# A new order of all steps, down to single second-layer matmuls, in a fused attention and feed-forward kernel

## The chip, the core and the metric

The kernel runs on one core of a Trainium2 chip. The core has five engines that each take their own instructions in the order in which the program issues them: TensorE (PE, matmuls; its weight loads are shown as PEld), VectorE (DVE), ScalarE (ACT), GpSimd (POOL) and SyncE (SP, which here only issues DMAs). The metric is the time on the device, in microseconds (us), as the median of several runs.

## The reference

There are two parts. Attention between a sequence `x` (8 batches, 8 heads, 512 positions, 64 features) and a small `state` (32 rows) runs both ways; its two results are put under each other (544 rows a batch), the heads side by side (512 columns), and a two-layer block with a periodic activation is applied to all 4352 rows:

```python
scores = scale * x @ state^T;   a  = softmax(scores);  xread = a @ state     # 512 rows a batch
scores2 = scale * state @ x^T;  a2 = softmax(scores2); sread = a2 @ x        # 32 rows a batch
X = concat([xread, sread]), heads to columns                                 # 4352 x 512
h = X @ w_in                                                                 # 512 -> 2048
g = h + sin(alpha * h)**2 / (alpha + 1e-9)
out = g @ w_out                                                              # 2048 -> 512
```

## The kernel before

The program is a long string, `ORDER`, of steps with their arguments, and a class `Steps` with a method for each. The body reads `ORDER` from left to right and calls the method; nothing is rearranged afterwards, so the string fixes the order on each engine, and the framework adds the waits that the data and the buffers need. A letter at a step's end chooses its engine (A ScalarE, V VectorE, G GpSimd). Eight PSUM banks are given out by hand: a step that opens a bank names it, and it waits until the bank's last user is done.

The work goes by batch. `xread @ w_in` is not computed as it stands: the softmax weights times (state times `w_in`) give the same, so for every batch a matrix M (256 x 2048) takes the place of `w_in`, and the first layer of 512 positions has a depth of 256.

- Loads: `li.s` and `lo.s` bring the four slices of `w_in` and `w_out` (slice s holds the columns or rows of f = 4s to 4s+3), `lx.b` the x of batch b, all from GpSimd's DMA queue, which turns them to bf16 on the way. `lq` brings the x of batch 0 from SyncE's queue and `xq` casts it.
- x transposed: for batch 0 by TensorE (`xtq`, copied by `xc`), for batch 1 by TensorE too (`xt`, `xc`), for batches 2 to 7 by a DMA (`td`) from a packed copy that `pk` makes.
- Scores and weights: `sc` (matmul), `ex` (exp), `rs`, `rr` (sum, reciprocal), `nm` (normalise: a multiply of two SBUF tensors), then a transpose of the weights: `at`, `ac` for batch 0, a DMA `ad` for the others.
- M: `m.b.s` makes a piece of 512 columns in two banks by 8 matmuls of 64 x 32 tiles; `me` casts it to bf16.
- First layer: `h.t.f` makes 128 of the 2048 columns for the 512 positions of batch t by two matmuls (`hg.t.f.g` is one of the two, used for batch 0). t = 8 stands for the state rows of all batches together (256 columns, four matmuls). Then `si` (sine, ScalarE), `sq` (square, any engine; a multiply of two SBUF tensors on VectorE and GpSimd), `gt` (VectorE; gives the bf16 tile gT and frees the bank of h).
- Second layer: `o.t.st.f0.f1` adds the products of f0 to f1-1 into the bank of 128 output rows (st); 16 make a tile. `oc` copies it to one of six buffers, `os` stores it from SyncE's queue. The last tile, t 7 st 3, is made in two parts of 384 and 128 columns (`oh`, `och`, `osh`).
- The other direction: `w`, `cs` (matmuls), `rc`, `xs` put the state rows' inputs together.
- `warm_up.n.cols.bank` issues n matmuls on zeros whose result nobody reads.

All matmuls of the second layer are recorded at line 587, those of `h` at 537 and 543 (t = 8), of `hg` at 552, of `m` at 488, of `xt` at 376; the squares and the normalisations at line 201 (a helper), `si` at 560, `gt` at 576, `me` at 496, `oc` at 595, `os` at 602 (605 for t = 8).

Of the kernel before, what the change touches and what calls it, by code (L numbers as in the profile page):

```python
# [33 lines left out]
me.1.1.1.A warm_up.2.128.2 gt.0.2 si.0.0 warm_up.2.128.2 warm_up.2.128.6 warm_up.2.128.3
warm_up.2.128.2 warm_up.2.128.6 me.0.1.0.A gt.0.1 sq.0.0.G m.0.2.3.2 si.0.3 m.1.2.5.6 hg.0.4.0.7
me.0.2.0.V me.0.2.1.A hg.0.4.1 sq.0.3.G hg.0.6.0.4 me.1.2.1.V hg.0.6.1 si.0.4 hg.0.7.0.3 hg.0.11.0.2
me.1.2.0.V si.0.6 hg.0.7.1 sq.0.4.G hg.0.5.0.6 gt.0.0 hg.0.5.1 si.0.7 hg.0.11.1 hg.0.8.0.5 hg.0.8.1
sq.0.6.A gt.0.3 sq.0.7.G o.0.3.0.2.0 si.0.5 gt.0.4 o.0.3.2.3 o.0.0.0.2.1 si.0.11 o.0.0.2.3 gt.0.6
sq.0.5.G o.0.0.3.4 o.0.2.0.1.7 si.0.8 o.0.3.3.5 sq.0.11.A gt.0.7 hg.0.9.0.4 sq.0.8.G o.0.2.1.2
gt.0.5 o.0.2.2.4 hg.0.9.1 gt.0.11 o.0.0.4.5 hg.0.10.0.3 si.0.9 o.0.2.4.5 gt.0.8 o.0.0.5.6 o.0.3.5.6  # L40
sq.0.9.A o.0.3.6.8 pk.1.0.V hg.0.10.1 xt.1.1.6 pk.1.1.V si.0.10 gt.0.9 xt.1.0.2 xc.1.1.0.A sq.0.10.G
o.0.2.5.6 xc.1.1.1.V xc.1.0.0.A o.0.0.6.7 xc.1.0.1.V o.0.0.7.8 o.0.2.6.7 sc.1.1.5 gt.0.10 sc.1.0.4
m.0.3.6.2 ex.1.0 o.0.2.7.8 me.0.3.0.V o.0.1.0.3.3 me.0.3.1.V o.0.1.3.6 hg.0.13.0.6 o.0.1.6.7 ex.1.1
rs.1.0 hg.0.13.1 m.1.3.2.4 si.0.13 o.0.1.7.8 rr.1.0 rs.1.1 nm.1.0.0.4.G o.0.1.8.9 hg.0.12.0.5
o.0.3.8.9 rr.1.1 hg.0.12.1 me.1.3.0.V o.0.0.8.9 nm.1.1.0.4.G o.0.1.9.10 o.0.0.9.10 me.1.3.1.V
si.0.12 o.0.0.10.11 o.0.3.9.11 sq.0.13.G ad.1 hg.0.15.0.2 sq.0.12.A o.0.1.10.12 hg.0.15.1 gt.0.12
o.0.2.8.10 si.0.15 o.0.2.10.11 gt.0.13 o.0.0.11.12 hg.0.14.0.4 sq.0.15.A hg.0.14.1 o.0.3.11.13
si.0.14 gt.0.15 o.0.0.12.13 o.0.1.12.13 o.0.3.13.14 sq.0.14.A pk.2.0.V o.0.1.13.14 pk.2.1.V h.1.2.5
gt.0.14 h.1.4.6 td.2 si.1.2 lx.3.0.1 h.1.0.2 si.1.4 o.0.0.13.15 sq.1.2.V h.1.1.4 si.1.0 gt.1.2
sq.1.4.G o.0.3.14.16 si.1.1 o.0.2.11.13 sq.1.0.A oc.0.3.V h.1.6.5 sq.1.1.G gt.1.4 o.0.2.13.14 os.0.3  # L50
h.1.3.0 si.1.6 gt.1.0 o.0.1.14.16 si.1.3 sq.1.6.G h.1.13.6 gt.1.1 oc.0.1.A o.0.2.14.15 o.0.0.15.16
si.1.13 h.1.15.2 sq.1.3.G lx.4.0.1 gt.1.6 os.0.1 o.0.2.15.16 oc.0.0.A h.1.5.4 sq.1.13.V oc.0.2.V
si.1.15 h.1.7.3 os.0.0 gt.1.3 o.1.1.0.1.5 si.1.5 os.0.2 h.1.8.1 sq.1.15.G gt.1.13 o.1.1.1.2 si.1.7
o.1.2.0.2.7 sq.1.5.A o.1.1.2.3 sq.1.7.G h.1.12.0 gt.1.15 si.1.8 h.1.9.6 gt.1.5 o.1.2.2.3 si.1.12
sq.1.8.G o.1.2.3.5 gt.1.7 si.1.9 o.1.1.3.4 h.1.10.2 sq.1.12.A pk.3.1.V h.1.11.4 sq.1.9.G gt.1.8
o.1.2.5.6 si.1.10 o.1.2.6.7 gt.1.12 h.1.14.3 si.1.11 sq.1.10.G o.1.2.7.8 gt.1.9 sc.2.1.1 si.1.14
o.1.1.4.7 sq.1.11.A pk.3.0.V sq.1.14.G o.1.1.7.8 gt.1.10 td.3 o.1.2.8.9 sc.2.0.0 o.1.1.8.9 gt.1.11
o.1.1.9.10 ex.2.0 o.1.3.0.2.6 gt.1.14 o.1.3.2.4 o.1.2.9.10 o.1.3.4.5 o.1.2.10.12 ex.2.1 o.1.2.12.13
rs.2.0 o.1.1.10.11 m.2.2.2.4.3.0 rr.2.0 rs.2.1 o.1.2.13.14 nm.2.0.0.4.G me.2.3.0.A o.1.2.14.15 w.0.1
rr.2.1 me.2.2.1.A me.2.3.1.V o.1.3.5.6 nm.2.1.0.4.G me.2.2.0.A o.1.3.6.7 o.1.2.15.16 cs.0 oc.1.2.A  # L60
m.2.0.3.4.0.2 ad.2 rc.0 o.1.3.7.8 me.2.1.1.A o.1.3.8.9 sc.3.0.7 xs.0.1 me.2.1.0.A o.1.1.11.12 os.1.2
me.2.0.0.V sc.3.1.2 me.2.0.1.A o.1.1.12.13 o.1.3.9.10 xs.0.0 pk.4.1.V pk.4.0.V td.4 o.1.3.10.11
ex.3.0 o.1.1.13.16 ex.3.1 rs.3.0 o.1.3.11.13 oc.1.1.A o.1.3.13.14 rr.3.0 h.2.0.0 rs.3.1 nm.3.0.0.4.G
os.1.1 o.1.3.14.16 si.2.0 rr.3.1 h.2.1.3 oc.1.3.V nm.3.1.0.4.G h.2.2.4 h.2.8.1 os.1.3 h.2.3.7 ad.3
si.2.2 o.1.0.0.3.2 si.2.8 sq.2.0.V o.1.0.3.4 sq.2.2.G gt.2.0 h.2.4.5 si.2.1 o.1.0.4.6 si.2.3
sq.2.8.G o.1.0.6.7 gt.2.2 h.2.9.6 si.2.4 o.2.3.0.1.0 o.1.0.7.8 sq.2.1.G o.1.0.8.9 sq.2.3.A gt.2.8
o.1.0.9.10 h.2.5.4 si.2.9 gt.2.3 o.1.0.10.11 sq.2.4.G o.1.0.11.12 si.2.5 h.2.7.1 gt.2.1 o.1.0.12.13
sq.2.9.A sq.2.5.G o.1.0.13.14 gt.2.4 o.1.0.14.15 si.2.7 o.1.0.15.16 o.2.0.0.1.7 gt.2.9 o.2.0.1.2
oc.1.0.A h.2.6.3 sq.2.7.G gt.2.5 o.2.3.1.2 os.1.0 o.2.3.2.3 si.2.6 h.2.10.5 o.2.3.3.4 sq.2.6.A
o.2.3.4.5 gt.2.7 h.2.11.6 si.2.10 h.2.12.2 gt.2.6 si.2.11 o.2.0.2.3 sq.2.10.G o.2.0.3.4 o.2.3.5.6  # L70
si.2.12 h.2.15.4 h.2.13.1 sq.2.11.A gt.2.10 sq.2.12.G o.2.0.4.5 si.2.15 h.2.14.3 gt.2.11 o.2.3.6.7
si.2.13 o.2.0.5.6 sq.2.15.G gt.2.12 o.2.0.6.8 si.2.14 o.2.3.7.9 sq.2.13.A o.2.3.9.10 gt.2.15
sq.2.14.G o.2.0.8.11 gt.2.13 o.2.0.11.12 sc.4.0.5 sc.4.1.6 gt.2.14 o.2.3.10.12 ex.4.0 o.2.3.12.13
w.1.2 cs.1 o.2.0.12.13 rc.1 o.2.3.13.15 ex.4.1 o.2.3.15.16 m.3.0.4.1.3.5 rs.4.0 oc.2.3.A o.2.0.13.14
me.3.1.0.A o.2.0.14.15 os.2.3 me.3.0.0.V o.2.1.0.1.6 me.3.0.1.A o.2.1.1.2 o.2.0.15.16 rr.4.0 rs.4.1
o.2.1.2.3 me.3.1.1.A nm.4.0.0.4.G h.3.1.0 oc.2.0.A o.2.1.3.4 rr.4.1 xs.1.0 m.3.2.3.4.1.5 si.3.1
nm.4.1.0.4.G os.2.0 xs.1.1 h.3.0.7 me.3.2.0.V h.3.2.2 ad.4 me.3.3.0.V o.2.1.4.6 lx.5.0.1 o.2.2.0.1.3
me.3.3.1.V si.3.2 o.2.2.1.3 si.3.0 h.3.6.1 sq.3.1.V sq.3.2.G me.3.2.1.V h.3.14.5 si.3.6 o.2.2.3.4
gt.3.1 o.2.2.4.5 sq.3.0.G si.3.14 o.2.2.5.7 gt.3.2 o.2.2.7.8 sq.3.6.A o.2.2.8.9 h.3.8.4 sq.3.14.G
gt.3.0 h.3.5.0 si.3.8 gt.3.6 h.3.15.2 si.3.5 o.2.2.9.10 sq.3.8.G gt.3.14 o.2.2.10.11 h.3.9.7 si.3.15  # L80
h.3.7.1 si.3.9 sq.3.5.G gt.3.8 o.2.2.11.13 si.3.7 h.3.10.5 sq.3.9.G o.2.2.13.14 sq.3.15.A gt.3.5
o.2.2.14.15 h.3.4.4 si.3.10 gt.3.15 o.2.1.6.7 sq.3.7.G o.2.1.7.8 si.3.4 o.2.2.15.16 o.2.1.8.10
sq.3.10.A gt.3.9 o.2.1.10.11 sq.3.4.G gt.3.7 o.2.1.11.13 oc.2.2.A o.2.1.13.14 gt.3.10 o.2.1.14.16
os.2.2 h.3.3.0 gt.3.4 oc.2.1.A h.3.12.2 si.3.3 pk.5.1.V o.3.2.0.1.7 os.2.1 m.4.2.1.3.5.6 pk.5.0.V
si.3.12 sq.3.3.V td.5 o.3.3.0.1.4 me.4.2.1.V me.4.2.0.A o.3.2.1.2 sq.3.12.G o.3.3.1.2 me.4.3.0.A
o.3.2.2.3 gt.3.3 o.3.3.2.3 h.3.11.1 me.4.3.1.A gt.3.12 h.4.10.3 si.3.11 h.4.9.5 si.4.10 h.4.12.0
sq.3.11.V h.4.11.6 si.4.9 gt.3.11 sq.4.10.G o.3.2.3.5 si.4.12 o.3.2.5.7 sq.4.9.A o.3.2.7.8 gt.4.10
sq.4.12.G o.3.2.8.10 si.4.11 o.3.2.10.11 gt.4.9 o.3.3.3.5 sq.4.11.A o.3.3.5.6 gt.4.12 o.3.3.6.8
m.4.0.2.1.3.5 gt.4.11 o.3.3.8.9 me.4.1.1.V me.4.0.1.A h.3.13.0 me.4.0.0.A h.4.8.6 me.4.1.0.V
h.4.15.1 si.3.13 h.4.2.5 si.4.8 sq.3.13.V h.4.1.2 lx.6.0.1 si.4.2 gt.3.13 o.3.2.11.12 o.3.1.0.2.3  # L90
si.4.15 o.3.1.2.3 sq.4.8.V o.3.1.3.4 sq.4.2.G si.4.1 gt.4.8 o.3.3.9.12 sq.4.15.A h.4.3.0 sq.4.1.G
gt.4.2 o.3.3.12.13 h.4.13.6 si.4.3 gt.4.15 o.3.3.13.15 si.4.13 sq.4.3.G o.3.3.15.16 gt.4.1 h.4.6.5
# [65 lines left out]
class Steps:  # L158
# [449 lines left out]
    def oh(k, t, st, half, bank):  # L608
        k.o(t, st, 0, k.FT, bank, half=half)
# [54 lines left out]
```

## Time and profile before

| | |
|---|---|
| median of 3 runs | 221.4 us (221.1 to 221.64) |
| the profiled execution | 221.22 us, its span 219.2 us |
| TensorE busy | 211.4 us (96%), 1593 matmuls recorded |
| ScalarE, VectorE, GpSimd busy | 173.4, 162.9, 106.2 us |
| granted TensorE clock | 1.00 |
| second-layer matmuls (L587) | 542 recorded, 133.9 us |
| squares and normalisations on GpSimd (L201) | 91, mean 1.02 to 1.06 us |
| loads | 17.4 MB read, about 200 GB/s moved until 40 us |

The span counts from the first to the last instruction; the rest of the profiled execution lies around it. Busy time of TensorE is the union of its matmuls, which overlap: a matmul of 512 columns is shown as 0.379 us, yet the next one starts 0.216 us after it. Some matmul records can be missing. A line of the timeline joins instructions of one form on one engine: start, length, engine, line, operation, tiles, and in brackets the idle time before and what ended it.

### The profile page before, as it was taken

The numbers are of one execution on the slowest core, as the hardware profiler recorded it, in microseconds if no ns is written. First come the engines' busy times: TensorE is split into PE (matmuls) and PEld (weight loads), VectorE is DVE, ScalarE is ACT, GpSimd is POOL, SyncE is SP. The second block draws the span as 40 slices with busy tenths as digits, with TensorE's granted clock in tenths as the row PEclk, the third lists the DMA queues.
The fourth block names the chain that finished last, engine by engine and source line by source line (L and its number), as shares of the span: only waits on it lengthen the run. The fifth ranks groups of instructions, "written<-read, shape, count | busy, mean of one in ns | idle before, by whom it ended". The sixth has DMA issues, their size and how long they took to land.

```text
span 219.2 us, 4303 instructions
## 1 busy us (share of the span) xinstructions
PE 211.4 (96%) x1593; PEld 104.5 (48%) x1619; DVE 162.9 (74%) x287; ACT 173.4 (79%) x297; POOL 106.2 (48%) x114
## 2 busy tenths in 40 slices
PE   7989999999999999999999999999999999999994
PEld 3744544444444534444454444454445555665452
DVE  3769996999787789989888788888667987661201
ACT  4799778997998979898996999798848896785111
POOL 5959533895195647753943387273501082121000
PEclk9999999999999999999999999999999999999999
DMA  6999999987491029167145327470220211012042
GB/s 195 178 206 204 205 204 146 217 169 133 101 238 48 3 92 143 57 144 96 48 79 131 109 71 96 134 110 0 48 100 0 98 48 48 0 51 96 1 143 96
DMA packets 38052, 23.48 MB, mean 107 GB/s; under 512 B 20992, under 2 KB 33680, under 8 KB 38032
## 3 DMA queue, kind: packets, MB, share of 16 engines
q1 hardware_dynamic: 26128, 15.08, 26.5%
q0 software_dynamic: 11648, 8.13, 26.0%
q8 instruction: 12, 0.20, 0.3%
q14 instruction: 8, 0.07, 0.1%
q10 hardware_dynamic: 256, 0.01, 0.1%
HBM read 17.44 MB, written 8.91 MB: 120 GB/s over the span
## 4 chain that ended last, share of the span: by engine, by line
PE 90%; DMA 6%; POOL 1%; issue 1%; ACT 0%
PE o_ps L587 54%; PE h_ps L537 22%; DMA w_in_sb<-in_moe_w_in_dram 5%; PE m_ps L488 4%; PE h_ps L543 3%; PE h_ps L552 2%; PE w_ps L450 2%; PE s_ps L399 2%; PE w_ps L461 1%; DMA s<-in_state_dram 1%; POOL w_in_sb L282 1%; PE x_ps L376 0%; POOL st_nat L267 0%; POOL s01b L255 0%; ACT o_sb L595 0%
## 5 line engine op out<-in xcount | busy, mean ns | idle before, releaser
L587 PE MATMUL o_ps<-w_out_sb,gT 128*128 128x512 bf16 (+2 forms) x542 | 133.9, 373 | 1.6 <-issue 1.0
L576 DVE SCALAR_TENSOR_TENSOR gT<-s,inva_sb,h_ps 128x512 bf16<-128x512 bf16 (+1 forms) x144 | 96.8, 713 | 20.4 <-POOL s L201 10.8
L201 POOL TENSOR_TENSOR s<-s 128x512 bf16<-128x512 bf16 (+1 forms) x75 | 75.9, 1022 | 64.4 <-ACT s L560 62.7
L560 ACT ACTIVATE s<-h_ps,alpha_sb 128x512 bf16<-128x512 f32 (+1 forms) x144 | 88.8, 670 | 11.1 <-PE h_ps L543 4.5
L587 PEld LDWEIGHTS <-gT 128*128 128x128 bf16 x560 | 52.3, 98 | 60.3 <-issue 5.0
L537 PE MATMUL h_ps<-AT,M 128*128 128x512 bf16 x219 | 60.0, 379 | 0.3
L537 PEld LDWEIGHTS <-M 128*128 128x128 bf16 x224 | 21.7, 98 | 25.9 <-issue 0.4
L569 ACT ACTIVATE s<-s 128x512 bf16<-128x512 bf16 (+1 forms) x53 | 31.4, 594 | 0.8
L201 POOL TENSOR_TENSOR A<-E,rR 128x512 bf16<-128x512 bf16 x16 | 16.6, 1056 | 23.8 <-ACT o_sb L595 12.9
L595 ACT COPY o_sb<-o_ps 128x512 f32<-128x512 f32 (+2 forms) x24 | 13.7, 570 | 16.6 <-PE o_ps L587 16.5
L496 ACT CAST M<-m_ps 128x512 bf16<-128x512 f32 x35 | 18.6, 594 | 8.2 <-PE m_ps L488 8.2
L496 DVE CAST M<-m_ps 128x512 bf16<-128x512 f32 x29 | 18.9, 679 | 2.5 <-PE m_ps L488 2.1
L595 DVE COPY o_sb<-o_ps 128x512 f32<-128x512 f32 x11 | 7.5, 685 | 12.9 <-PE o_ps L587 12.9
L201 DVE TENSOR_TENSOR s<-s 128x512 bf16<-128x512 bf16 (+1 forms) x16 | 7.0, 439 | 6.2 <-ACT s L560 6.1
L410 DVE TENSOR_REDUCE R<-E 128x16 f32<-128x512 bf16 x16 | 10.4, 657 | 0.7 <-ACT E L406 0.6
L488 PE MATMUL m_ps<-w_in_sb,stT 64*32 64x512 bf16 x256 | 10.2, 382 | 0.1
L468 DVE RECIPROCAL rC<-w_ps 128x128 f32<-128x128 f32 x8 | 7.6, 948 | 3.3 <-PE w_ps L461 3.2
L303 PE MATMUL warm_ps<-warm 128*128 128x128 bf16 (+3 forms) x66 | 8.6, 271 | 1.4 <-DVE warm L209 1.2
L552 PE MATMUL h_ps<-AT,M 128*128 128x512 bf16 x29 | 8.4, 379 | 0.9 <-ACT M L496 0.7
L406 ACT ACTIVATE E<-s_ps 128x512 bf16<-128x512 f32 x16 | 8.8, 602 | 0.4 <-PE s_ps L399 0.4
L543 PE MATMUL h_ps<-xs_all,w_in_sb 128*128 128x256 bf16 x64 | 9.1, 273 | 0.0
L543 PEld LDWEIGHTS <-w_in_sb 128*128 128x128 bf16 x64 | 6.3, 98 | 3.4
(56 smaller groups left out, 101.8 us busy)
## 6 DMA issues: line engine op xcount, KB each, us to landing
out_dram<-o_sb SPq DMA_DIRECT2D x33, 256.0 KB, 2.3
xnat<-in_x_dram POOLq DMA_DIRECT2D x7, 512.0 KB, 7.5
w_in_sb<-in_moe_w_in_dram POOLq DMA_DIRECT2D x4, 512.0 KB, 10.9
w_out_sb<-in_moe_w_out_dram POOLq DMA_DIRECT2D x4, 512.0 KB, 18.0
x<-in_x_dram SPq DMA_DIRECT2D x4, 256.0 KB, 4.2
st_nat<-in_state_dram POOLq DMA_DIRECT2D x1, 256.0 KB, 5.3
out_dram<-o_sb SPq DMA_DIRECT2D x1, 192.0 KB, 1.9
s<-in_state_dram SPq DMA_DIRECT2D x1, 128.0 KB, 2.2
```

The lines of the kernel that those rows point to most:

```text
L201: {"V": k.nc.vector, "G": k.nc.gpsimd}[eng].tensor_tensor(out, a, b, ALU.mult)
L410: k.nc.vector.reduce_sum(R[:, g], k.t["E", b][:, g].rearrange("p c (h j) -> p (c h) j", j=k.Ns), axis=AX.X)
L488: k.nc.tensor.matmul(k.t["m", b, s + n, g][o0:o0 + k.Ns, :], k.stT[k.half(r), b * k.G + g, c0:c0 + k.Ns], k.w_in_sb[k.half(r), 2 * g + h, ...
L496: k.copy(eng)(k.t["M", b][:, g, s * k.FW:(s + 1) * k.FW], k.t["m", b, s, g][:])
L537: k.nc.tensor.matmul(hp[:, :n], k.t["M", t][:, g, fs], k.t["AT", t][:, g, :], start=(g == 0), stop=(g == k.G - 1),)
L543: k.nc.tensor.matmul(hp[:, :n], k.w_in_sb[:, q, fs], k.xs_all[:, q].rearrange("p b j -> p (b j)"), start=(q == 0), stop=(q == k.Q - 1),)
L552: k.nc.tensor.matmul(k.t["h", t, f][:], k.t["M", t][:, g, f * k.P:(f + 1) * k.P], k.t["AT", t][:, g, :], start=(g == 0), stop=(g == k.G - 1),)
L560: k.nc.scalar.activation(s[:, :n], k.t["h", t, f][:, :n], ACT.Sin, scale=k.alpha_sb[:, f:f + 1])
L569: k.nc.scalar.activation(s2[:, :n], s[:, :n], ACT.Square)
L576: k.nc.vector.scalar_tensor_tensor(gT[:, :n], k.t["s2", t, f][:, :n], k.inva_sb[:, f:f + 1], k.t["h", t, f][:, :n], ALU.mult, ALU.add,)
L587: k.nc.tensor.matmul(k.t["o", t, st, half][:, cols], k.t["gT", t, f][:, rows], k.w_out_sb[:, f, cols], start=(f == 0), stop=(f == k.FT - 1),)
L595: k.copy(eng)(o_sb[:, cols], k.t["o", t, st, half][:, cols])
```

## The change

`ORDER` is written anew from the first step to the last. The steps compute the same. What differs:

- `o` now is a single matmul, `o.t.st.f`, and `oo.t.st.bank` opens the bank; the sixteen f of a tile may come in any order, mixed with other work. The first one issued starts the sum and the sixteenth ends it (`k.made` counts). `ho` and `hg` do the same for the first layer of batch 0.
- `xt` transposes two heads at once from the packed copy, 16 transposes of 128 x 128 for 32 of 128 x 64; so `pk.1` now comes ahead of it.
- Warm-up matmuls: 15 in place of 66, most of them of 512 columns.
- The engines of some steps: squares on VectorE 46 (16 before), ScalarE 35 (53), GpSimd 63 (75); normalisations on VectorE 4 (0), on GpSimd 12 (16); casts of M on ScalarE 42 (35), VectorE 22 (29); copies of output tiles on ScalarE 25 (22), VectorE 8 (11); casts of batch 0's x on VectorE 2 (0) and ScalarE 2 (4).
- The places of all steps on all queues: among them the loads of `w_out` and of batch 1's x, which GpSimd issues behind the normalisations of batch 0; the loads of batches 2 to 4; the sine table's first load (`sin_table`), right behind the second exp; and the stores, many of them long after their copy. At the end the 128 columns of the last tile come first and the 384 last.

```diff
-zero.1 identf.V lq.3.S s01_c.G l_st li.0 xq.0.A s01_t.4 li.1 xtq.0.5 warm_up.1.384.3 xq.1.A
...
-sc.0.1.0 li.3 st_t.0.3 ex.0.1 rr.0.0 st_t.1.4 lo.2 st_c.0.0.V st_c.0.1.A warm_up.2.128.5
...
+zero.1 identf.V lq.3.S s01_c.G ho.0.0.0 ho.0.2.1 s01_t.2 l_st s01_k.0.V xq.1.V s01_k.1.V xq.0.A
...
+sc.0.1.2 ex.0.1 sin_table li.2 rs.0.0 rr.0.0 rs.0.1 rr.0.1 nm.0.0.0.4.G st_t.0.4 st_c.0.0.A st_t.1.3
+st_c.1.0.V nm.0.1.0.4.G st_c.0.1.A warm_up.3.512.7 at.0.0.2 ac.0.0.V warm_up.1.512.7 m.0.0.5.6
+me.0.0.0.A warm_up.1.512.7 at.0.1.2 m.1.0.4.7 ac.0.1.V st_c.1.1.V lo.0 me.1.0.1.V me.0.0.1.A
+hg.0.2.0 hg.0.2.1 me.1.0.0.A si.0.2 sq.0.2.V ho.0.6.6 lo.1 ho.0.1.2 hg.0.1.1 hg.0.1.0 hg.0.0.0
+lx.1.0.1 m.0.1.4.3 hg.0.0.1 me.0.1.0.V si.0.1 me.0.1.1.A li.3 sq.0.1.G m.1.1.7.5 hg.0.6.1 si.0.0
...
+sq.0.6.G m.0.2.5.3 me.0.2.1.A sq.0.0.V gt.0.1 ho.0.4.2 hg.0.4.1 hg.0.4.0 gt.0.0 m.1.2.7.0 ho.0.8.3
+hg.0.8.1 me.0.2.0.V hg.0.8.0 ho.0.9.5 hg.0.9.1 si.0.3 sq.0.3.G hg.0.9.0 me.1.2.0.A me.1.2.1.V si.0.4
+sq.0.4.A ho.0.11.7 hg.0.11.1 si.0.5 lo.2 hg.0.11.0 gt.0.6 oo.0.1.0 o.0.1.1 gt.0.3 si.0.11 ho.0.7.6
...
-o.7.0.8.9 oc.8.1.A o.7.0.9.10 oc.8.0.V o.7.0.10.12 os.8.1 o.7.0.12.13 os.8.0 o.7.0.13.16 o.7.2.0.2.2
-oc.7.0.A o.7.2.2.5 os.7.0 o.7.2.5.11 oh.7.3.0.1 o.7.2.11.13 och.7.3.0.A o.7.2.13.15 osh.7.3.0
-o.7.2.15.16 oh.7.3.1.4 oc.7.2.V os.7.2 och.7.3.1.A osh.7.3.1
...
+o.8.0.3 o.8.1.4 o.8.0.1 o.8.0.6 o.7.1.2 o.8.0.14 o.8.0.11 oc.8.0.V oc.7.1.A o.8.1.3 os.7.1 o.8.1.11
+os.8.0 o.8.1.2 o.8.1.9 o.8.1.10 oc.8.1.A oh.7.3.1.5 os.8.1 och.7.3.1.A osh.7.3.1 oh.7.3.0.1
+och.7.3.0.A osh.7.3.0
...
     def xt(k, b, g, bank):
         tp = k.t["xt", b, g] = k.ps(bank, [k.P, 2, k.S], BF16, "x_ps")
         for h in range(2):
             for i in range(k.C):
-                for r in range(2):
-                    k.nc.tensor.transpose(
-                        tp[k.half(r), h, i * k.P:(i + 1) * k.P],
-                        k.t["xnat", b][:, 2 * (2 * g + h) + r, i * k.D:(i + 1) * k.D],
-                        k.ident[:],
-                    )
+                k.nc.tensor.transpose(
+                    tp[:, h, i * k.P:(i + 1) * k.P], k.pair(b, i, 2 * g + h), k.ident[:]
+                )
...
+    def oo(k, t, st, bank, half=None):
+        k.t["o", t, st, half] = k.ps(bank, [k.P, k.DOUT], FP32, "o_ps")
+        k.made["o", t, st, half] = 0
+
+    def o(k, t, st, f, half=None):
         cols = k.cols(half)
...
+        k.made["o", t, st, half] += 1
+        k.nc.tensor.matmul(
+            k.t["o", t, st, half][:, cols], k.t["gT", t, f][:, rows], k.w_out_sb[:, f, cols],
+            start=k.made["o", t, st, half] == 1, stop=k.made["o", t, st, half] == k.FT,
+        )
```

## The prediction

> **What bounds the kernel now.** I read the page first, then the list of waits, then the timeline at the front, around the narrow matmuls and at the tail. The page (busy times; 40 slices; chain):
>
> ```profile
> PE 211.4 (96%) x1593; PEld 104.5 (48%) x1619; DVE 162.9 (74%) x287; ACT 173.4 (79%) x297; POOL 106.2 (48%) x114
> ...
> PE   7989999999999999999999999999999999999994
> ...
> PEclk9999999999999999999999999999999999999999
> ...
> PE 90%; DMA 6%; POOL 1%; issue 1%; ACT 0%
> ```
>
> TensorE is full from the fourth slice to the last, at the whole clock, and carries 90% of the chain; the rest is the loading of weights. A busy share can hide waits, so I turn it into a stream rate. The timeline, in four answers (the front, 25 to 31 us, 51 to 54 us, the tail):
>
> ```profile
> 18.20 2.54 PE L552 MATMUL h_ps<-AT,M 128*128 128x512 bf16 x11 [0.16 <-issue]
> ...
> 20.57 2.32 PE L587 MATMUL o_ps<-w_out_sb,gT 128*128 128x512 bf16 x10
> ...
> 25.32 0.38 PE L552 MATMUL h_ps<-AT,M 128*128 128x512 bf16 x1
> 25.63 1.08 PE L376 MATMUL x_ps<-ident,xnat 128*64 128x128 bf16 x32
> ...
> 28.18 0.41 PE L488 MATMUL m_ps<-w_in_sb,stT 64*32 64x512 bf16 x8
> 28.52 1.68 PE L587 MATMUL o_ps<-w_out_sb,gT 128*128 128x512 bf16 x7
> ...
> 53.28 0.63 PE L488 MATMUL m_ps<-w_in_sb,stT 64*32 64x512 bf16 x16
> 53.84 0.61 PE L587 MATMUL o_ps<-w_out_sb,gT 128*128 128x512 bf16 x2
> ...
> 214.18 0.48 ACT L595 COPY o_sb<-o_ps 128x384 f32<-128x384 f32 x1 [4.39 <-PE o_ps L587]
> 215.26 0.69 DVE L595 COPY o_sb<-o_ps 128x512 f32<-128x512 f32 x1 [7.09 <-PE o_ps L587]
> 216.15 0.27 ACT L595 COPY o_sb<-o_ps 128x128 f32<-128x128 f32 x1 [1.50 <-PE o_ps L587]
> ```
>
> Eleven h matmuls from 18.20 to 20.57 are 0.2158 us each, although one is shown as 0.379: the difference, 0.165, is the time until its result is out. One h matmul before the transposes takes 25.63-25.32 = 0.31, so entering a column-tiled mode costs 0.09. One piece of M alone takes 28.52-28.18 = 0.34, two in a row 53.84-53.28 = 0.56, so the second one 0.22.
>
> Everything from the first second-layer matmul (20.57), counted from the order: 528 o and 236 h at 0.2158 = 164.87; 16 h of the state rows at 0.436 (four of 256 columns) 6.98; the last o tile in 16 pieces of 384 and 16 of 128 columns 3.49; 14 sc at 0.232, 8 w at 0.466, 8 cs (one directly behind another) = 9.62; 26 pieces of M in 14 runs = 14x0.34+12x0.22 and the way out 7.48; 17 entries at 0.093 1.58; the transposes of x 1.03+0.09 = 1.12. Sum 195.1, so 215.7; the last matmul's slot ends at 215.96 (its copy starts at 216.15, less 0.03 and 0.165). In 195 us the stream stands still for 0.26. What can change the time is therefore: when the stream starts, how long it is, how often it stops, and what follows it (3.25 us to the span's end at 219.2). The profiled execution took 221.22, its span and 2.0 around it, 0.2 under the median of 221.4.
>
> **The change, part by part.**
>
> Stream: -0.55. The number of matmuls of every kind is the same but for the transposes and warm-ups. The transposes go from 32 half-width ones (1.12 with entry) to 16 of full width, which need no column tiling: 26 warm-ups of that shape ran in 1.62, less 0.22 for the last and over 25 steps 0.056 each, so 0.90: -0.22. M: 13 runs in place of 14, 15 entries for 17: -0.13-0.19 = -0.32. Single o matmuls in any order cost what runs cost: in both orders every matmul loads its own weights, and alternating h and o keep 0.216 (22.73, 22.94, 23.59 in the timeline).
>
> Front: -0.4. Before the first o both orders do 20 h matmuls and 6 pieces of M, so the two starts compare directly. The loads are the clock: the waits and the issue-to-landing times put slices of w_in at 11.8 (4.11+7.7), 14.9, 17.4 and 27.65 (8.65+19.0) and the first slice of w_out at 19.9 (6.31+13.6). The new order issues w_out and x of batch 1 on GpSimd only after the two normalisations, from about 11.8 in place of 6.3; transfers of the queue follow one another at 2.55 us, the queue holds slices 1 and 2 until 17.4, so they land as before. Without that cover each load would come later by the gap. After 17.4 TensorE has two pieces of M in separate runs (0.45 each with entry) and 8 h: 2.62, so 20.0 at best, and not before 19.9. I walked ScalarE's queue at start-to-start times (sine 0.57, cast 0.48): the sine table is now loaded right behind the second exp, at about 9.5, not at 11.62, so the first cast of M is done at 12.9 and the first complete h at 13.7; then casts and sines follow without a gap to the cast that frees the bank of the last h before the first o, at 19.7. TensorE reaches M's first piece 0.2 late, and the second waits 0.1 for the bank of h 0. First o at 20.2 (20.57 before). Bounds: 19.95 by w_out, 20.8 if ScalarE slips by one operation.
>
> Tail: +0.3. The last piece is now the one of 384 columns: its copy takes 0.48 for 0.27, its 192 KB land in 1.9 for 1.8. The state rows' stores (issue 207.87) now come some 3 us before the last one; before, two of them and the next store were through by 214.2. The last one waits for them by 0 to 0.3; I take 0.
>
> Stores and loads moved: stores are issued up to 40 us after their copy. There are six buffers; the least distance from a store to the copy that reuses its buffer is 4 us of stream against 2.3 to land: nothing. x of batches 2 to 4 is now issued together behind batch 1's normalisation (31.7); lands at 35.4, 38 and 40.5 by the same 2.55; batch 3's packing is in VectorE's queue at 39.9, with batch 1's products behind it: covered by 1.9. ad.1 starts at some 32.2 with 3.3 to land, 35.5; its first h stands at 35.8: covered by 0.3. A normalising multiply on VectorE, on that path, isn't in the trace: between a square's 0.34 spacing and a gT's 0.66; I take 0.6 (it reads float scales, like the gT), so the cover is 0 to 0.6. xq on VectorE lies likewise between 0.42 (a bf16 copy) and 0.69 (a cast from PSUM); both end before 11.8.
>
> Stops: 0.26 as before, up to 2. The stream stops when a bank or a gT isn't ready. For each bank I counted the stream between the producer's last matmul and the next owner, less the chain (result 0.165, sine 0.69, square 0.42 VectorE, 0.64 ScalarE, 1.04 GpSimd, gT 0.74, hand-overs 0.03). Under 0.3 us of slack: 4 places before, 39 now; under zero: none beyond 0.02. So the order fits, with little room.
>
> No other engine becomes the bound: VectorE gains 30 squares (10.3 at 0.34) and 4 normalisations (2.4) and loses 7 casts and 3 copies (6.0), 163 to 170 busy; ScalarE loses 18 squares (9.4 at 0.52) and gains those ten (4.8), 173 to 169. What could use up the room is the port. VectorE does 46 squares in place of 16 and 4 normalisations; GpSimd 75 operations for 91.
>
> ```profile
> 59.95 2.05 POOL L201 TENSOR_TENSOR A<-E,rR 128x512 bf16<-128x512 bf16 x2 [4.52 <-ACT o_sb L595]
> ...
> 61.62 0.66 DVE L201 TENSOR_TENSOR s<-s 128x512 bf16<-128x512 bf16 x1 [0.41 <-ACT s L560]
> ```
>
> A square of 0.42 took 0.66: it came while GpSimd multiplied (to 62.00) and ended 0.28 after that. By this row a square that meets a GpSimd multiply ends 0.28 behind it. Of the 46, 18 follow a GpSimd square in ScalarE's order (6 of 16 before), about ten of them within 0.9 us; they lose 0.05 to 0.5 each, and of the five with under 0.27 slack only one (t 4, f 15) has a multiply beside it. By the row that is 0 to 0.2 on the stream; I keep 0 and put it in the range.
>
> The Trainium skill speaks against this part: GPSIMD Engine Reference, Key points, says that GpSimd shares its SBUF interfaces with VectorE and contends with VectorE instructions that have two SBUF inputs. It gives no price; if all 18 lost a quarter of a microsecond and half of that reached TensorE, the sum would be 2.2 higher.
>
> **Sum.** 20.2+194.6+0.26+3.55 = 218.6 of span, 0.6 under 219.2; on the median's scale 220.8. The forecast's own range: 220.3 (start at 19.95, stops of 0) to 220.95 (0.2% under the median).
>
> **The rivals.** About 0.2% (0.44 us) is what a measurement can tell from no change.
>
> Slower, by stops: the slack that fell from 4 to 39 places under 0.3 is spent by VectorE squares that wait for GpSimd. For: the row at 61.62, and a full stream never wins a stop back. Against: the zero of overdrawn places. At 0.05 for each of the 39, 2.0: 222.8. It decides from 1.0 us of stops on, since 0.6 is in hand and 0.44 must be passed.
>
> No change: the start comes at 20.6 (ScalarE slips by one cast) and the stops are 0.1 more: 0.5 less gain, 221.3. For: ScalarE's chain and TensorE's meet at 19.7 to the tenth. Against: the same rows held in the front before.
>
> Slower, by the clock: 66 warm-ups become 15; the first seven took 3.17, 0.43 each, twice the later rate. If the clock fell back before 12 us, the first pieces of M and 9 h would run at half rate, 1.5 longer: 222.3. Against: in the new order no gap before 12 is over 1.5.
> The Trainium skill, TensorE: Matmul & The Clock Gate, the HAM clock gate, wants a whole idle window of about 3.4 us before the rate halves; by it this costs nothing.
>
> **The numbers.** Forecast 0.46, no change 0.27, slower by stops 0.22, by the clock 0.05. The range reaches from 220.3, just past the best start, to 222.4, most of the way into the stops.
>
> **What would show it.** Right: the first o at 20.0 to 20.4, the transposes 16 in about 0.9, the last copy 128x384, TensorE's idle after 20 under 0.5. Wrong: waits of o_ps or h_ps matmuls for VectorE (gT, M) of over 1 us together, squares on VectorE well over 0.42, or a first o after 20.6.

## The result, and the profile after

The changed kernel took 233.17 us (median of 6 runs, 232.66 to 235.16) against 221.32 for the kernel before (221.1 to 221.64): a ratio of 1.0555, 95% interval 1.0508 to 1.0602. It is 5.6% slower; the forecast was 220.8, its range 220.3 to 222.4. The profiled execution took 232.93 us, its span 230.8.

From the page after: busy times, TensorE in 40 slices, its granted clock, and the chain by engine.

```profile
PE 213.7 (93%) x1526; PEld 102.2 (44%) x1552; DVE 178.1 (77%) x314; ACT 171.8 (74%) x286; POOL 89.1 (39%) x98
...
PE   7889993798899999999999999999999999999993
...
PEclk9999998599999999999999999999999999999999
...
PE 63%; DVE 13%; DMA 10%; ACT 7%; POOL 3%; issue 2%; ACTq 0%; SPq 0%
```

Before, no slice between the third and the last was under 9. Now the seventh is 3, and the clock falls with it. TensorE's share of the chain has fallen from 90% to 63%; VectorE now has 13% of it and DMAs 10%. The list of TensorE's waits (total us, times, longest) names the slice's owner:

```profile
PE h_ps L536 <- DMA AT<-A: 5.4, 1, 5.4
...
PE o_ps L591 <- DVE gT L578: 1.0, 3, 0.6
```

The wait in the timeline: the three loads of x, issued in one go by GpSimd, beside `ad.1`, the transpose of batch 1's weights; then the last second-layer matmuls and the first eight of batch 1.

```profile
32.39 2.70 POOL L277 DMA_DIRECT2D xnat<-in_x_dram  x3
...
33.07 1.34 SPq L439 DMA_TRANSPOSE AT<-A  x1
...
34.56 2.11 PE L591 MATMUL o_ps<-w_out_sb,gT 128*128 128x512 bf16 x9
...
42.05 3.59 PE L536 MATMUL h_ps<-AT,M 128*128 128x512 bf16 x8 [5.38 <-DMA AT<-A]
```

TensorE had work until 36.5 and stood until 42.05. The eight matmuls behind the wait are 0.42 apart (3.59 less the 0.63 that one is shown with, over 7 steps) where 0.216 is normal. Each of the DMA tables below ends in the median time from issue to landing; the window is 31 to 46 us after, and 31 to 47 before.

```profile
xnat<-in_x_dram POOLq DMA_DIRECT2D x3, 512.0 KB, 9.5
AT<-A SPq DMA_TRANSPOSE x1, 8.9
```

And the kernel before, the same table:

```profile
AT<-A SPq DMA_TRANSPOSE x1, 3.5
```

The transpose that took 3.5 there takes 8.9 now. The table by stretches (busy us of each engine, then the granted clock, the DMA share and GB/s) has the clock at 0.50 for the 3.7 us that follow the wait; the record has it at 0.5 from 38.86 to 45.69, so it fell 2.2 us after the end of TensorE's last matmul (36.67):

```profile
36.50:42.00 5.50, 0.17 (x1) 0.00 (x0) 1.23 (x3) 0.00 (x0) 0.00 (x0) 0.71 1.42 180
42.00:45.70 3.70, 3.65 (x9) 1.34 (x10) 1.78 (x4) 2.08 (x4) 0.04 (x1) 0.50 1.13 154
```

The forecast's span was 218.6; the profiled one is 12.2 longer, and the trace says where. The first second-layer matmul is at 20.24 (+0.04). From it to the last one it is 206.5 us, where the forecast makes 194.8 of the 195.3 before: +11.7, of which 5.55 are the wait for `ad.1` (the 5.38 of the row, and 0.165 by which a matmul is shown longer than its slot), 1.8 the half clock (nine matmuls in 3.74 instead of 1.94), and 4.4 are left for all other stops. The tail, from the last matmul's start to the end, is 4.05 for 3.31: +0.74, of which 0.3 was forecast.

Most of the other stops are waits for VectorE, 2.1 us of them for gT between 51 and 60. VectorE's timeline shows what held gT up; the second number is the length of the group.

```profile
49.50 1.59 DVE L350 COPY xp<-xnat 128x1024 bf16<-128x1024 bf16 x2
...
54.97 1.11 DVE L203 TENSOR_TENSOR s<-s 128x512 bf16<-128x512 bf16 x1
...
56.78 1.66 DVE L350 COPY xp<-xnat 128x1024 bf16<-128x1024 bf16 x2
```

Two packing copies took 0.76 together before; here 1.59 and 1.66. A square of 0.42 took 1.11. GpSimd multiplied beside each. Over the whole trace I added up what these operations took above their length alone (copy 0.415, square 0.42, normalisation 0.69; only excesses over 0.06): 0.57 us before (three operations), 5.96 after (2.89 on six of 14 copies, 2.23 on eight of 46 squares, 0.84 on three of four normalisations).

### The profile page after: what moved, and what is told of

It is laid out like the page before. It is cut to its first block, busy times and chain, and to the rows that moved or that the text cites. A ratio compares the mean times of both kernels' runs of the same rounds, so it can differ in the third digit from the quotient of the medians.

```text
span 230.8 us, 4133 instructions
## 1 busy us (share of the span) xinstructions
PE 213.7 (93%) x1526; PEld 102.2 (44%) x1552; DVE 178.1 (77%) x314; ACT 171.8 (74%) x286; POOL 89.1 (39%) x98
## 4 chain that ended last, share of the span: by engine, by line
PE 63%; DVE 13%; DMA 10%; ACT 7%; POOL 3%; issue 2%; ACTq 0%; SPq 0%
PE o_ps L591 38%; PE h_ps L536 15%; DVE gT L578 5%; DMA w_in_sb<-in_moe_w_in_dram 5%; DMA AT<-A 4%; PE h_ps L542 3%; ACT s L562 3%; PE m_ps L487 3%; POOL s L203 2%; DVE xp L350 2%; DVE s L203 1%; PE h_ps L554 1%; PE s_ps L398 1%; DVE R L409 1%; DMA s<-in_state_dram 1%
## 5 line engine op out<-in xcount | busy, mean ns | idle before, releaser
L591 PE MATMUL o_ps<-w_out_sb,gT 128*128 128x512 bf16 (+2 forms) x539 | 137.0, 373 | 2.5 <-DVE gT L578 1.0
L203 POOL TENSOR_TENSOR s<-s 128x512 bf16<-128x512 bf16 (+1 forms) x63 | 62.8, 1005 | 83.4 <-ACT s L562 78.9
L536 PE MATMUL h_ps<-AT,M 128*128 128x512 bf16 x221 | 64.1, 388 | 6.2 <-DMA AT<-A 5.4
L203 POOL TENSOR_TENSOR A<-E,rR 128x512 bf16<-128x512 bf16 x12 | 12.5, 1050 | 44.2 <-issue 17.7
L203 DVE TENSOR_TENSOR s<-s 128x512 bf16<-128x512 bf16 (+1 forms) x46 | 21.2, 461 | 10.7 <-ACT s L562 10.1
L495 ACT CAST M<-m_ps 128x512 bf16<-128x512 f32 x42 | 22.5, 595 | 5.8 <-PE m_ps L487 5.8
L571 ACT ACTIVATE s<-s 128x512 bf16<-128x512 bf16 (+1 forms) x35 | 21.1, 605 | 1.0
L495 DVE CAST M<-m_ps 128x512 bf16<-128x512 f32 x22 | 14.3, 686 | 1.6 <-PE m_ps L487 1.4
L554 PE MATMUL h_ps<-AT,M 128*128 128x512 bf16 x31 | 9.1, 381 | 0.5 <-DVE M L495 0.4
L599 DVE COPY o_sb<-o_ps 128x512 f32<-128x512 f32 x8 | 5.5, 687 | 4.3 <-PE o_ps L591 4.3
L350 DVE COPY xp<-xnat 128x1024 bf16<-128x1024 bf16 x14 | 8.4, 620 | 0.0
```

The source lines that it names most:

```text
L203: {"V": k.nc.vector, "G": k.nc.gpsimd}[eng].tensor_tensor(out, a, b, ALU.mult)
L350: k.copy(eng)(k.t["xp", b][:, :, hs, :], k.t["xnat", b][:, hs, :].rearrange("p h (i d) -> p i h d", i=k.C),)
L495: k.copy(eng)(k.t["M", b][:, g, s * k.FW:(s + 1) * k.FW], k.t["m", b, s, g][:])
L536: k.nc.tensor.matmul(hp[:, :n], k.t["M", t][:, g, fs], k.t["AT", t][:, g, :], start=(g == 0), stop=(g == k.G - 1),)
L571: k.nc.scalar.activation(s2[:, :n], s[:, :n], ACT.Square)
L591: k.nc.tensor.matmul(k.t["o", t, st, half][:, cols], k.t["gT", t, f][:, rows], k.w_out_sb[:, f, cols], start=k.made["o", t, st, half] == 1 ...
```

## The experiments

Theory A: the loads beside `ad.1` held it up. Theory B: VectorE's waits for GpSimd make the other stops. C: something else. All times are medians; the kernel before, run beside each experiment, took 221.07 to 221.37. Only the places of steps are shown of each edit.

**1. The loads away from the transpose** (a_loads_apart).

```diff
- sq.0.11.G                      ...  nm.1.1.0.4.G ad.1 lx.2.0.1 ... lx.3.0.1 ... sq.0.14.V ... lx.4.0.1
+ sq.0.11.G lx.2.0.1             ...  nm.1.1.0.4.G ad.1          ... sq.0.14.G lx.3.0.1 lx.4.0.1
```

> The changed kernel, with x of batch 2 loaded behind the last slice of w_out (sq.0.11.G, about 23 us) and x of batches 3 and 4 issued only behind a square of batch 0 (sq.0.14 on GpSimd in place of VectorE, about 37 us), so that no load is issued within a microsecond of the transpose ad.1 (33.07). Theory A (the three loads held ad.1 up): ad.1 lands at 36.5 as in the kernel before, the 5.5 us wait of the first h of batch 1 is under 0.3, the clock stays whole, and of 233.2 go 5.5 and the 1.8 of nine matmuls at half rate: 225.9 (225.2 to 226.6). Theory B (the rest of the order can't keep that pace: VectorE and GpSimd hold each other up, and a stream that arrives earlier waits at the same gT): half of it or more comes back as waits behind 47 us: 229.5 or more. Theory C (ad.1 is late for a reason of its own): 233.

Measured: 226.94 us (226.61 to 227.84), ratio 1.025, interval 1.0213 to 1.0287. Its DMA table and timeline:

```profile
AT<-A SPq DMA_TRANSPOSE x1, 3.5
```

```profile
36.76 1.91 PE L531 MATMUL h_ps<-AT,M 128*128 128x512 bf16 x8
...
46.09 0.39 PE L586 MATMUL o_ps<-w_out_sb,gT 128*128 128x512 bf16 x1 [1.60 <-DVE gT L573]
```

`ad.1` takes 3.5 again, the wait is gone and the clock of the profiled execution stays whole. The time is 0.3 above A's range and well below the 229.5 of B. So A is shown: of the 7.35 us (5.55 of wait and 1.8 of half clock), 6.2 come off. But 1.1 came back in the way that B had it, though not in its size: the stops for gT between 44 and 53 now add up to 3.4 us, where the same steps stopped for 2.1 in the changed kernel. Between 42 and 53 VectorE's copies and squares took 3.4 longer than alone (two copies from 42.94 took 2.44).

**2. Only two of the loads away** (a_two_later): `lx.2` stays where it was, 0.7 us ahead of `ad.1`; `lx.3` and `lx.4` move as in 1.

> The changed kernel, with x of batch 2 where it is (issued at 32.4, 0.7 ahead of ad.1) and only x of batches 3 and 4 issued later, behind sq.0.14 on GpSimd (about 37 us). Theory A1 (a transpose starts to move only when the load issued ahead of it is nearly through): the load lands at about 37.0, ad.1 at 38.5 to 39, the wait is 2 to 2.5 us, and the clock stays whole: 233.2 less 3.3 less 1.8, 228.1 (227 to 229). Theory A2 (ad.1 shares its time with the loads issued behind it, and the one ahead costs little): ad.1 at 36.5 to 37, 226.0. Theory C: 233.

Measured: 230.34 us (229.24 to 231.26), ratio 1.0395, interval 1.0349 to 1.0441; `ad.1` landed 6.8 us after its issue.

```profile
39.48 3.60 PE L531 MATMUL h_ps<-AT,M 128*128 128x512 bf16 x8 [3.29 <-DMA AT<-A]
```

The stop, counted in the same way as the 5.55, was 3.45 us, and the clock fell this time too, for 6.8 us in the profiled execution. A1 had foreseen a wait of 2 to 2.5 and a whole clock: the median lies outside its range, and further still from the 226.0 of A2. When the packets of the transpose begin to move tells more: 1.28 us behind its issue in the kernel before and in a_loads_apart, 3.74 here, 3.60 in the changed kernel. The load ahead alone thus costs some 3.3 of the 5.4 us. That it must be nearly through first, as A1 says, is not borne out: some 600 of its 1024 packets had moved by then. The two loads behind the transpose go with the other 2.1, which fits sharing: between 39.5 and 41.0 of the changed kernel's trace, 375 packets of loads and 354 of the transpose moved, about one for one.

The Trainium skill, DMA: Bandwidth & Descriptors, Queues, rings and completion order, says that a DMA engine takes turns between its queues by packets. The 375 and 354 fit that; the late first packet is not explained by it, and no run here says why it is late.

**3. The wait kept, TensorE kept busy in it** (a_kept_warm).

```diff
- h.1.3.6
+ warm_up.24.512.6 h.1.3.6
```

> The changed kernel with 24 warm-up matmuls of 512 columns (5.2 us at full rate) ahead of the first h of batch 1, in the bank that this h takes, so that TensorE is busy while it waits for ad.1. The wait itself stays: ad.1 still lands at 42.0. If the halved clock (0.5 from 38.86 to 45.69 in the profile) is a consequence of the idle time and costs the stream 1.8: 231.4, and no row of the clock at 0.5 about 40. If the halved clock costs nothing further or has another cause: 233.2.

Measured: 232.82 us (232.45 to 232.97), ratio 1.0506, interval 1.0474 to 1.0539. The clock stayed whole from 11 us on, through the wait and behind it, so the idle time was what lowered it there; yet only 0.35 of the 1.8 came off. The timeline shows where the rest went:

```profile
42.49 1.90 PE L531 MATMUL h_ps<-AT,M 128*128 128x512 bf16 x8 [0.42 <-DMA AT<-A]
...
51.83 0.39 PE L586 MATMUL o_ps<-w_out_sb,gT 128*128 128x512 bf16 x1 [1.61 <-DVE gT L573]
```

The stream arrived earlier at the gT that VectorE delivers late, and stopped there 1.77 us instead of 0.42. Behind the wait VectorE, not TensorE's clock, set the pace.

**4. The loads beside the transpose, in the kernel before** (b_loads_beside).

```diff
- lx.2.0.1 ... nm.1.1.0.4.G                             ... sq.0.13.G ... ad.1 ... lx.3.0.1 ... lx.4.0.1
+          ... nm.1.1.0.4.G lx.2.0.1 lx.3.0.1 lx.4.0.1  ... sq.0.13.V ... ad.1
```

> The kernel before, with one thing of the change alone: x of batches 2, 3 and 4 issued together behind the normalisation of batch 1 (about 33 us), right beside ad.1; sq.0.13 goes from GpSimd to VectorE so that GpSimd's squares do not queue behind the three issues. Theory A: ad.1 lands at about 42 in place of 36.5, the first h of batch 1 waits some 5.2 us and the clock halves: 221.3 + 5.2 + 1.8 = 228.3 (227.3 to 229.3). Theory B or C (the loads are not the cause): 221.3 to 222.

Measured: 225.46 us (225.18 to 227.53), ratio 1.0177, interval 1.0141 to 1.0213. The loads beside the transpose, almost without the rest of the change (one square changes its engine), cost 4.1 us; their size I had too high by 2.8. The profiled execution is the slowest of the five (227.53): its first second-layer matmul came at 21.58, and its clock was 0.5 for one step of 3.41 us behind the wait, while three of the others had a whole clock.

```profile
41.27 1.46 PE L532 MATMUL h_ps<-AT,M 128*128 128x512 bf16 x6 [3.13 <-DMA AT<-A]
```

`ad.1` landed 7.2 us after its issue. Here the first load went out only 0.08 ahead of it, and the transpose's first packet moved after 1.39 us: so it was not held back at its start, and its length fits the sharing alone. In its order TensorE also had work until 37.98.

The kernel before had such a case of its own. The table of its whole trace has the seven transposes of weights at a median of 3.3:

```profile
AT<-A SPq DMA_TRANSPOSE x7, 3.3
```

One of the seven, issued at 81.59, 0.08 behind a load of 512 KB, took 6.7. TensorE did not wait for it. On the other hand the load of batch 2's x, issued at 15.2, was still moving until 35.39 beside `ad.1` (33.03), which took only 3.5 there: what counts is not merely that a load is under way.

**5. The packing copies out of GpSimd's way, first try** (a_copies_apart): a_loads_apart with

```diff
- gt.0.14                   ... pk.2.0.V ... pk.2.1.V pk.3.0.V ... gt.1.13 ... sq.1.7.V gt.1.7 ... pk.4.0.V ... pk.3.1.V td.3
+ gt.0.14 pk.2.0.V pk.2.1.V ... gt.1.13 pk.3.0.V pk.3.1.V td.3 pk.4.0.V ... sq.1.7.V gt.1.7
```

> The kernel of a_loads_apart (226.9, span 225.1), with the packing copies of batches 2 to 4 on VectorE moved out of the time in which GpSimd multiplies: both of batch 2 right behind gt.0.14 (about 38 us), those of batch 3 and the first of batch 4 behind gt.1.13, where GpSimd issues a load and then waits. Nothing else is moved but td.3, which reads the copies. In a_loads_apart five copies took 0.48, 1.26, 1.26, 0.48 and 1.26 in place of 0.41 each, every one of them ending 0.28 behind a multiply of GpSimd, and two squares 0.58 and 1.11 in place of 0.42; the stream stopped for 3.4 us for gT between 44 and 53. Theory B1 (the copies wait for GpSimd's multiplies, and gT, the stream's feed, behind them): the copies take 0.41 again, and most of the 2.6 lost on them comes off the stops: 224.4 (223.8 to 225.2). Theory B2 (VectorE simply has too much work in that stretch, wherever the copies lie): 226.5 to 227.5, with the stops elsewhere.

Measured: 226.53 us (225.53 to 228.06), ratio 1.0231, interval 1.0198 to 1.0264: not distinguishable from 226.94, so as a forecast B1 missed; the time lies at the lower edge of B2's range. The trace shows half of it kept and half undone:

```profile
38.09 0.75 DVE L345 COPY xp<-xnat 128x1024 bf16<-128x1024 bf16 x2
...
47.73 1.93 DVE L345 COPY xp<-xnat 128x1024 bf16<-128x1024 bf16 x3
49.58 1.25 DVE L198 TENSOR_TENSOR s<-s 128x512 bf16<-128x512 bf16 x1
```

The first two copies are back at 0.75, and the stop at 44 is gone. The other three I had put ahead of `sq.1.7` and `gt.1.7`; the third and the square met GpSimd again, and TensorE waited 2.6 us from 49.1 for that gT. The clock of the profiled execution was 0.5 for a step behind this wait and for another at 7.8 to 11.2. Three of its six runs, the profiled one among them, had a lower mean clock (0.985 to 0.992) and took 227.24 to 228.06, the other three 225.53 to 225.83.

**6. Second try** (a_copies_spread).

```diff
- gt.0.14                   ... pk.2.0.V ... pk.2.1.V pk.3.0.V ... sq.1.7.V gt.1.7 ... pk.4.0.V ... pk.3.1.V td.3 ... sq.1.15.G ... pk.4.1.V
+ gt.0.14 pk.2.0.V pk.2.1.V ... sq.1.7.V gt.1.7 pk.3.0.V pk.3.1.V td.3 ... sq.1.15.A ... pk.4.1.V pk.4.0.V
```

> a_loads_apart again with the packing copies moved, now so that few of them meet a multiply of GpSimd and none stands ahead of a gT that TensorE is about to need: both of batch 2 behind gt.0.14 as in a_copies_apart, those of batch 3 (and td.3) behind gt.1.7, the first of batch 4 beside its second one, and sq.1.15 on ScalarE in place of GpSimd. In a_copies_apart the first two copies took 0.75 together and the stop at 44 was gone, but three copies and a square in a row ahead of gt.1.7 took 1.93 and 1.25 and stopped the stream for 2.6 at 48.8. Theory B1 (VectorE's wait for GpSimd's multiplies makes the stops): stops of under 1.0 between 37 and 56 together, no half clock, 223.9 (223.2 to 224.8). Theory B2 (too much work for VectorE in that stretch): 225.5 or more.

Measured: 224.49 us (224.0 to 224.8), ratio 1.0146, interval 1.0129 to 1.0164.

```profile
41.60 0.59 PE L531 MATMUL h_ps<-AT,M 128*128 128x512 bf16 x2 [0.19 <-DVE gT L573]
...
53.52 0.41 PE L482 MATMUL m_ps<-w_in_sb,stT 64*32 64x512 bf16 x8 [0.22 <-DVE gT L573]
```

The stops between 37 and 56 add up to 0.9 (0.36, 0.11 and 0.39 are the ones over 0.1), the clock stayed whole, and the time is inside B1's range: 2.45 us off (2.15 when each kernel is taken against the kernel before that ran beside it), with the same work on VectorE but for where it lies. So it is not the amount of work. The edit does two things at once, though: the copies meet fewer multiplies (above their length alone they took 0.66 us in all, 3.31 in a_loads_apart), and none stands ahead of a gT that is about to be needed. What each of the two gives is not shown. VectorE's excess over the whole trace fell from 6.3 to 3.2 us.

**7. The operations by themselves** (port_alone).

> Leaves out the whole computation and stores zeros: it measures VectorE's operations by themselves, first with GpSimd idle (6 copies, 6 squares, 4 normalising multiplies, 4 gT, 4 casts from PSUM, 4 sums), then the same while GpSimd does 30 multiplies of 128x512 in a row, then 8 copies while GpSimd issues three loads. Theory B1: a copy takes 0.41 and a square 0.42 alone, and 1.0 to 1.3 each beside the multiplies, each ending 0.28 behind a multiply; the normalising multiply goes the same way; gT (0.71), casts (0.68) and sums (0.66) stay as they are. Rival: everything that VectorE does grows by a like share, or copies by under 0.2. Of the copies beside the issues of loads nothing is expected; 0.41 if only multiplies are in the way.

VectorE's timeline; the upper rows with GpSimd idle, the lower ones while it multiplied:

```profile
4.70 1.35 DVE L201 COPY xp<-xn 128x1024 bf16<-128x1024 bf16 x3
5.96 2.71 DVE L203 TENSOR_TENSOR s<-s 128x512 bf16<-128x512 bf16 x6
8.60 2.86 DVE L206 TENSOR_TENSOR a<-s,r 128x512 bf16<-128x512 bf16 x4
11.58 3.10 DVE L210 SCALAR_TENSOR_TENSOR a<-s,inva_sb,warm_ps 128x512 bf16<-128x512 bf16 x4
...
20.44 6.32 DVE L201 COPY xp<-xn 128x1024 bf16<-128x1024 bf16 x6
26.68 7.15 DVE L203 TENSOR_TENSOR s<-s 128x512 bf16<-128x512 bf16 x6
33.76 5.86 DVE L206 TENSOR_TENSOR a<-s,r 128x512 bf16<-128x512 bf16 x4
39.65 3.10 DVE L210 SCALAR_TENSOR_TENSOR a<-s,inva_sb,warm_ps 128x512 bf16<-128x512 bf16 x4
```

One by one in the trace: a copy goes from 0.427 to 1.145, a square from 0.425 to 1.146, a normalising multiply from 0.69 to 1.41; each copy and square ends 0.28 behind the end of a GpSimd multiply, each normalising multiply 0.55 behind. gT (0.747), casts from PSUM (0.69) and sums (0.686) don't change. Beside GpSimd's issues of loads three copies took 0.67, 0.87 and 0.83. The first copy of the lower group began before GpSimd did and took 0.42.

The Trainium skill, GPSIMD Engine Reference, Key points, names two kinds of VectorE instruction that contend: those with two SBUF inputs and those in a 2-port performance mode. The prediction had passed over the second kind. That the copies are of it is the skill's account (VectorE: DVE Perf Modes, What auto-detection actually checks, gives such a mode to copies from SBUF to SBUF); the runs show only that they wait as the squares do.

**8. Two more stops, and the tail.** a_waits_apart is a_copies_spread with `xs.3.0` ahead of `nm.6.0` and `oc.4.3` ahead of `pk.7.0`.

> a_copies_spread (224.5, span 223.0) with two operations of VectorE taken from behind an operation that waits for GpSimd: xs.3.0, which the matmul at 130.8 waits for (0.53), goes ahead of the normalisation nm.6.0 (1.16 there, 0.69 alone), and the copy oc.4.3, which the matmul at 140.6 waits for (0.29), goes ahead of the packing copy pk.7.0 (0.87 there, 0.42 alone). If VectorE's waits for GpSimd make these stops too, both are gone: 0.82 less, 223.7 (223.4 to 224.1). Rival: the stream then meets the next late gT within a few us and keeps its end: 224.3 to 224.7.

Measured: 225.71 us (224.36 to 226.48), ratio 1.0177, interval 1.014 to 1.0214. No gain; the median lies above both forecasts. Both stops are gone (0.82 together), and two others for gT stand in their place, 0.35 at 133.4 and 0.77 at 143.5, as the rival had it. The profiled execution, the slowest of six, lost another 1.4 us in a wait for `ad.2`, which was 0.3 in a_copies_spread; why is not shown.

a_tail_swapped adds the old order of the last tile's parts:

```diff
- oh.7.3.1.5 os.8.1 och.7.3.1.A osh.7.3.1 oh.7.3.0.1 och.7.3.0.A osh.7.3.0
+ oh.7.3.0.5 os.8.1 och.7.3.0.A osh.7.3.0 oh.7.3.1.1 och.7.3.1.A osh.7.3.1
```

> a_waits_apart with the two parts of the last tile in the order of the kernel before: the 384 columns first, the 128 last. The tail (last matmul's start to the end of the span) was 3.31 before and 4.05 after. Theory: the narrow last copy gives 0.21 and the shorter last matmuls 0.11; the landing gives little, since the store of tile 7 st 1, queued behind the state rows', lands only 0.5 ahead of the last one and then sets the end: 0.3 to 0.5 less than a_waits_apart. If the width of the last part is all there is: 0.74 less. If the state rows' stores alone set the end: 0 to 0.1 less.

Measured: 224.68 us (223.97 to 225.08), ratio 1.0139, interval 1.0105 to 1.0172, and a tail of 3.66 for 4.03, so 0.37 less: the first theory. The last two stores land at 221.08 and 221.27. The median fell by 1.0, more than the tail gives; in the profiled execution the wait for `ad.2` is 0.3 again.

**9. The transposes alone, in the kernel before** (b_full_width).

```diff
- pk.1.0.V hg.0.10.1 xt.1.1.6 pk.1.1.V          (32 transposes of 128 x 64)
+ hg.0.10.1 pk.1.1.V xt.1.1.6 pk.1.0.V          (16 of 128 x 128)
```

> The kernel before, with the change to the transposes of batch 1's x alone: 16 of 128 x 128 from the packed copy in place of 32 of 128 x 64, and the copy pk.1.1 ahead of the first of them. As the prediction had it: 0.22 off the stream, 221.1 (220.9 to 221.4). Rival: the transposes now wait for a copy of 0.4 that starts only when x of batch 1 has landed (25.1): 0 to 0.4 of wait, so 221.2 to 221.7.

Measured: 221.51 us (221.01 to 222.9, 12 runs), ratio 1.0008, interval 0.9993 to 1.0024: no change. The 16 took 0.89 (25.17 to 26.06 in the trace) where the 32 took 1.12 with their entry, as priced. The scores that need their result then waited 0.07 and 0.24 for the copies `xc`, against 0.09 before: from the first transpose to the next piece of M it is 2.65 us in place of 2.55. The gain was hidden by the chain behind it.

No version tried beats the kernel before. The best, a_copies_spread and a_tail_swapped, are 1.4 to 1.5% slower. In a_copies_spread 3.7 us of stops are left, of which about 1.5 end with a gT, 0.8 with the two operations of experiment 8, 0.6 lie in the chain of batch 1's transposes, and 0.5 end with `ad.1` or `ad.2`; the rest are shorter ones. How much of these VectorE's waits for GpSimd cause stays open: 8 shows that taking away two of them isn't enough.

## Why the prediction was wrong, point by point

- **The step that failed first: "ad.1 starts at some 32.2 with 3.3 to land, 35.5; its first h stands at 35.8: covered by 0.3".** The 3.3 is the median of the transposes in the kernel before. `ad.1` had no load issued within 0.9 us of it there; the one transpose of that trace that did, at 81.59, took 6.7. The median was kept although the same paragraph moved three loads of 512 KB to exactly that place. With them it was 8.9, and the stop, forecast at nothing, 5.55. The loads' own times failed likewise: "lands at 35.4, 38 and 40.5" took 2.55 a load from a queue that was already moving; they landed at 39.5, 42.8 and 45.4. The wait belonged among the rivals: a transpose that stands behind a load.
- **The clock.** The rival looked for it in the front, at the warm-ups; in the changed kernel it fell at the wait. By itself that cost little, since VectorE was late there anyway (experiment 3). The front was not safe either: in two of the eight profiled executions with this front (a_kept_warm, a_copies_apart) the clock was 0.5 for one step, from 7.6 or 7.8 on. Their first second-layer matmul still came at 20.47 and 20.48, so this did not cost the 1.5 us of the rival.
- **"0.26 as before, up to 2" for the stops; port "0 to 0.2".** 4.4 us. The rule that I read off the square at 61.62 (it ends 0.28 behind the multiply) is the right one for copies and squares (0.28 in port_alone too); what failed was where I applied it. I went through the 46 squares for direct hits on their own gT, and left out the 14 copies, 0.4 long and met by multiplies of 1.04, and what is queued behind them: every gT of VectorE. A slack that is counted with each chain alone says nothing of an engine that serves all chains in one queue. The normalising multiply, taken at 0.6, is 0.69 long alone and was 0.87 beside GpSimd on the path of `ad.1`. The rival "slower, by stops" had this mechanism and half its price.
- **Front: right in the mean, not settled.** 20.24 for a forecast of 20.2. Eight profiled executions with this front have 19.66 to 20.76, mean 20.29; three with the old one 20.20, 20.57 and 21.58.
- **Transposes: priced right, worth nothing** (experiment 9): I subtracted them from the stream without asking what is late next.
- **Tail: mis-sized, 0.74 for 0.3.** The last matmuls of 384 columns and their copy give 0.32 of it. The rest is landing: the last store landed 2.26 after its issue, behind the state rows' and the next one, which itself took 4.45 (224.96 to 229.41). The text had this at "0 to 0.3" and took 0.

## What to carry to other kernels

A landing time read from a trace holds for the neighbours that the DMA had there: where a change moves a load next to a transfer with 0.3 us of cover, take the transfer to land about as late as the load itself (`ad.1` landed 0.5 ahead of the load next to it in b_loads_beside, 0.6 behind it in a_two_later and 2.6 behind it in the changed kernel). When slack is counted for a new order, walk the busiest in-order engine as one queue, with every operation at the length it has beside its neighbours; an operation that ends with GpSimd's multiply delays all that stands behind it. Removing one stop from such a stream can simply show the next one, as in experiment 8.

## What the runs showed of the hardware

- A DMA transpose (`ad.1`) on SyncE's queue, issued 0.68 us behind a 512 KB load from GpSimd's queue, moved its first packet 3.6 to 3.75 us after its issue; issued 0.08 behind one (b_loads_beside), or with none issued in the 0.7 us ahead (the kernel before, a_loads_apart), 1.28 to 1.39. From issue to landing it took 3.5 where no load was issued within 0.9 us of it, and 6.8 to 9.2 with one to three loads close to it (a_two_later, b_loads_beside, the changed kernel, a_kept_warm).
- The clock halved after idle times that were no whole window. In a_copies_apart TensorE stood for 2.5 us (49.2 to 51.7), and the clock was 0.5 from 52.17 to 55.58, one step of 3.41 us in the record. In the changed kernel it fell when TensorE had stood for 2.2 us. The Trainium skill, TensorE: Matmul & The Clock Gate, the HAM clock gate, has the clock fall after an idle window of about 3.4 us; the step's length agrees, the need for a whole idle window does not. A stop of 1.6 us (a_loads_apart) left the clock whole.
- GpSimd's operations grow too where VectorE's meet them: a multiply of 1.04 took 1.10 beside copies and squares, and 1.37 beside normalising multiplies (port_alone).
